# Attention feeding two gated layers: VectorE's copies, lower halves and a weight conversion moved between steps

## The chip, the core and the metric

The kernel runs on one core of a Trainium2 chip. The core has TensorE (matmuls, written to PSUM banks of 128 x 512 fp32), VectorE, ScalarE and GpSimd (elementwise work; GpSimd does not read PSUM here) and SyncE, which issues nearly all DMAs. Each engine works through its own list of instructions in order and waits on semaphores for the others. The metric is the device time of one execution in microseconds (us).

## What is computed

The reference is causal attention over 2 batches of 12 heads, 448 positions of 64, and two layers behind it, all in fp32:

```python
scores = scale * np.matmul(q, k.transpose(0, 1, 3, 2))
scores = np.where(mask, -1000000000.0, scores)
scores = scores - np.max(scores, axis=-1, keepdims=True)
attn = np.exp(scores)
attn = attn / (np.sum(attn, axis=-1, keepdims=True) + 1e-09)
x = np.matmul(attn, v)                      # heads joined: 896 x 768
x = (x @ w_a) * (x @ w_b) @ w_out           # d_ff 1536
h = x @ w_in                                # d_ff 2048
out = (h * (1.0 / (1.0 + np.exp(-h)))) @ w_out2
```

## The kernel before, in words

**Attention** is a hand-written pipeline of 30 steps (the loop at L705). Two heads make one unit `u`, 12 units in all, the first six of batch 0 (b = 0). A unit takes two steps, d = 2u (even, i = 0) and d = 2u + 1 (odd, i = 1). The queries of a unit are cut into seven chunks `j`; the even step handles chunks 6, 5, 0 (448, 384 and 64 keys), the odd one 4, 1, 3, 2. In a step TensorE does, in this order: the scores of unit u into banks `sc` (L568 and L572), a part of the product with v of an earlier unit (`xo`, L654, five steps later than its scores), and the transposes of normalized rows into two banks `pt` (L642, two steps later than their scores). Scores use a split of q and k in two parts: GpSimd makes the upper halves `qh`, `kh` (L538), VectorE the lower ones `ql`, `kl` (L543), in the odd step for the next unit.

For each chunk VectorE takes scores to `sm` with scale, mask and row minimum `nmax` (L591, one pool of three buffers, one for a group of chunks), ScalarE makes `p` = exp and its row sums (L595). A step later VectorE adds epsilon and inverts (`sums`, `rcp`, L604 and L605), and GpSimd multiplies `p` with it (L608). The step after that, TensorE transposes `p`; a step later still the banks `pt` are copied to `ptr` (L737 in the trace, where deferred work is called) by the table `COPIES`: those of an even step by one ScalarE and three VectorE copies, those of an odd one by three ScalarE copies. Transposes take their two banks from three, from unit 8 on from two (L621). Finished `xo` of a unit is cut in an upper part `xh` and a copy `xf` on ScalarE and a lower part `xl` on VectorE (L383 to L389).

**What sets the order.** `defer(k, prio, fn)` puts work k steps ahead; at the end of a step its list is sorted by `prio` and issued (L736). Before, ScalarE's copies have priority 0, `finish` of x 1, score work 2, VectorE's copies and `normalize` 3, and lower parts `xl` follow from `tasks`. Behind all that, a timeline issues steps of **weight conversion** by due time (L743). A granule of weights comes as 8-byte words; ScalarE makes `wr` from them (L213, L219), VectorE joins them to fp32 `wq` (L225, L230), then both make halves `wgah`/`wgal`, `wgbh`/`wgbl` (L252, L256). `CONV0`, `CONV1`, `CONV2` say in half steps over which stretch granules 0 and 1 are converted: 8 to 34 and 35 to 52. Sums of blocks of x (`S`, with halves `p3` to `p7`; L391) also run there, from step 22 on.

**After attention** come the layers, all matmuls `acc` of 448 columns (L295). Steps 24 to 27 already hold 36 matmuls of granule 0 on batch 0, the early products. Granule 0's other 36 follow attention, then 72 of granule 1, then granule 2 with halves `wah`, `wal`. The end of the kernel copies the last bank in two halves, on ScalarE and VectorE, and stores each (L933 to L938).

Of the kernel before, what the change touches and what calls it, by code (L numbers as in the profile page):

```python
# [24 lines left out]
    ((0, "scalar", 0, 2, 5, 2), (1, "vector", 2, 1, 5, 2), (1, "vector", 3, 1, 6, 1), (1, "vector", 0, 1, 0, 1)),  # L25
    ((0, "scalar", 0, 1, 1, 4), (1, "scalar", 1, 1, 2, 3), (1, "scalar", 2, 1, 4, 1)),
)
LAG_T = 2
# [3 lines left out]
CONV1 = 34  # L32
CONV2 = 52
# [6 lines left out]
A1 = 38  # L40
A2 = 11
# [21 lines left out]
def fused_kernel(ctx: ExitStack, tc: tile.TileContext, qk, v, w_ab, w_mid, w_in, w_out, out):  # L63
# [315 lines left out]
    def arrive(b, chunk, src):  # L379

        hi, lo = A.new(F32R, "xh"), A.new(F32R, "xl")
        XS[chunk, b] = hi, lo
        nc.scalar.copy(out=hi, in_=src)  # L383
        XF[chunk, b] = t = A.new(F32, "xf")
        nc.scalar.copy(out=t, in_=src)
        c, i = divmod(chunk, 2)
        if (b, i) != (1, 0):
            ACTS[{(0, 0): 1, (0, 1): 2, (1, 1): 4}[b, i]][c] = hi, lo
        return lambda: nc.vector.tensor_tensor(out=lo, in0=src, in1=hi[:].bitcast(F32), op=ALU.subtract)  # L389

    def sums_of(c):  # L391


        a11, a12, a21, a22 = (XF.pop((2 * c + i, b)) for b in range(B) for i in range(2))
# [11 lines left out]
        s3 = add("S", a11, a21, ALU.subtract)  # L406
        yield 2
# [69 lines left out]
    with tc.manual_schedule():  # L477

        with ExitStack() as actx:
# [6 lines left out]
            sm_p = sctx.enter_context(right(name="sm_p", bufs=3))  # L486
# [126 lines left out]
            def transposes(u, i):  # L613
# [11 lines left out]
                for n, copy, kb, nkb, j, nj in COPIES[i]:  # L625
                    size = nkb * nj * 2 * D
                    src = bank[n][:, o[n]:o[n] + size].rearrange("p (k h q) -> p k h q", k=nkb, h=2)
                    o[n] += size
                    dst = t["pt"][:, kb:kb + nkb, :, j * D:(j + nj) * D]
                    for a in range(nkb):  # L630
                        for c in range(nj):
                            place[j + c, kb + a] = src[:, a, :, c * D:(c + 1) * D]
                    if nkb == 1:
                        src, dst = src[:, 0], dst[:, 0]
                    if copy == "vector":
                        defer(1, 3, partial(nc.vector.tensor_copy, out=dst, in_=src))
                    else:
                        defer(1, 0, partial(nc.scalar.copy, out=dst, in_=src))
# [22 lines left out]
            tasks = []  # L661

            def finish(b, chunk, src):
                tasks.append(arrive(b, chunk, src))
                if b == 1 and chunk % 2:
                    sums_x.gens.append(sums_of(chunk // 2))
# [38 lines left out]
            for d in range(n_steps):  # L705
# [32 lines left out]
                while tasks:  # L738
                    tasks.pop(0)()
# [5 lines left out]
            for fn in sorted(late):  # L745
                for _, f in late[fn]:
                    f()
            while tasks:
                tasks.pop(0)()
# [126 lines left out]
        for at, g in enumerate(granules):  # L876
# [36 lines left out]
            def ending(b, i, acc, m=m, last=last):  # L913
# [19 lines left out]
                if last and b == 1 and i == 1:  # L933
                    o2, half = A.new(F32, "o2"), S // 2
                    nc.scalar.copy(out=o[:, 0:half], in_=src[:, 0:half])
                    nc.vector.tensor_copy(out=o2[:, 0:half], in_=src[:, half:S])
                    nc.scalar.dma_start(out=out[m + i, :, b * S:b * S + half], in_=o[:, 0:half])
                    nc.sync.dma_start(out=out[m + i, :, b * S + half:(b + 1) * S], in_=o2[:, 0:half])  # L938
                    A.free(o2)
                else:  # L940
                    nc.scalar.copy(out=o, in_=src)
                    nc.sync.dma_start(out=out[m + i, :, toks[b]], in_=o)
# [54 lines left out]
```

## Time and profile before

| | |
|---|---|
| time, median of 3 runs | 566.44 us (566.26 to 568.65) |
| the profiled execution: its time, its span | 566.35 us, 564.5 us |
| busy: TensorE, VectorE, ScalarE, GpSimd | 553.8, 426.6, 376.7, 72.8 us |
| granted TensorE clock | full speed in all slices |
| chain that ended last | TensorE 89%, of it 82% matmuls `acc`; VectorE 5% |

Busy time is a mean over very different stages: attention ends near 104 us, and GpSimd works only there. Matmuls overlap and their ends are modelled, so a busy TensorE need not be at its peak; how long the same instructions take in one place and in another says more. In brackets behind a timeline row stands how long the engine was idle before it, and who ended that.

### The profile page before, as it was taken

Reading aid. Unit: us, or ns where it says so; the run is one execution under the profiler, and the core shown is the slowest. Engines: PE = TensorE matmul, PEld = TensorE weight load, DVE = VectorE, ACT = ScalarE, POOL = GpSimd, SP = SyncE. Lnnn points to the kernel's source line nnn. Section 1 sums busy time; section 2 is a strip of 40 time slices with the busy share of each in tenths; the row PEclk is TensorE's granted clock in tenths of the full one; section 3 lists DMA queues with packets and bytes.
Section 4 is the critical chain, followed back from the end, with each engine's and each line's share of the span. In section 5 each row is a group of like instructions: output and inputs, shape, how many; then the busy total and the mean of one; then the engine's idle time right before and its main releaser. Section 6 shows DMA issues by size and latency. Waiting matters only on the chain.

```text
span 564.5 us, 8382 instructions
## 1 busy us (share of the span) xinstructions
PE 553.8 (98%) x2978; PEld 493.7 (87%) x2978; DVE 426.6 (76%) x818; ACT 376.7 (67%) x730; POOL 72.8 (13%) x127
## 2 busy tenths in 40 slices
PE   8999989999999999999999999999999999999997
PEld 6667757899999999999999999999999999999996
DVE  5899898688989898879683788888886797442500
ACT  4989988756666666678563675877776995632601
POOL 5888865000000000000000000000000000000000
PEclk9999999999999999999999999999999999999999
DMA  7346423033343433333333333333333242631501
GB/s 248 118 128 191 123 60 147 1 113 111 113 145 137 156 120 113 113 113 111 113 112 113 111 113 111 113 111 113 118 120 118 74 138 87 212 106 49 174 1 65
DMA packets 18234, 65.42 MB, mean 116 GB/s; under 512 B 2192, under 2 KB 6928, under 8 KB 18192
## 3 DMA queue, kind: packets, MB, share of 16 engines
q1 hardware_dynamic: 18048, 64.77, 34.1%
q8 instruction: 23, 0.38, 0.3%
q14 instruction: 19, 0.16, 0.1%
q10 hardware_dynamic: 144, 0.11, 0.1%
HBM read 62.13 MB, written 2.75 MB: 115 GB/s over the span
## 4 chain that ended last, share of the span: by engine, by line
PE 89%; DVE 5%; issue 2%; POOL 2%; ACT 1%; DMA 1%; SPq 0%; DVEq 0%; ACTq 0%; POOLq 0%
PE acc L295 82%; PE pt L642 2%; DVE sm L591 2%; PE sc L568 2%; POOL p L608 2%; PE xo L654 1%; PE sc L572 1%; DVE ptr L737 1%; DVE kl L543 1%; DMA k<-qk 1%; ACT p L595 0%; DVE sums L604 0%; ACT ptr L737 0%; SPq L526 0%; DVE wgal L256 0%
## 5 line engine op out<-in xcount | busy, mean ns | idle before, releaser
L225 DVE SCALAR_TENSOR_TENSOR wq<-wr 128x768 uint32<-128x768 uint32 (+1 forms) x76 | 66.3, 875 | 25.5 <-ACT wr L219 24.8
L318 ACT COPY s<-acc 128x448 f32<-128x448 f32 x72 | 38.5, 534 | 61.0 <-PE acc L295 60.6
L219 ACT ACTIVATE wr<-wr,wbias 128x768 uint32<-128x768 uint32 (+1 forms) x76 | 69.8, 918 | 0.0
L213 ACT ACTIVATE wr<-wr 128x768 f32<-128x768 f32 (+1 forms) x76 | 63.8, 839 | 2.5 <-DMA wr<-w_out 1.3
L230 DVE SCALAR_TENSOR_TENSOR wq<-wr,wq 128x768 uint32<-128x768 uint32 (+1 forms) x76 | 64.2, 877 | 0.1
L608 POOL TENSOR_SCALAR p<-p,rcp 128x448 f32<-128x448 f32 (+6 forms) x84 | 56.9, 693 | 19.5 <-DVE rcp L605 13.7
L595 ACT ACTIVATE p<-sm,nmax 128x448 f32<-128x448 f32 (+6 forms) x84 | 42.1, 514 | 13.0 <-DVE nmax L591 13.0
L295 PE MATMUL acc<-th,wgbl 128*128 128x448 f32 x168 | 49.5, 366 | 0.0
L295 PE MATMUL acc<-th,wgbh 128*128 128x448 f32 x168 | 49.4, 366 | 0.0
L295 PE MATMUL acc<-tl,wgah 128*128 128x448 f32 x168 | 49.4, 366 | 0.0
L295 PE MATMUL acc<-th,wgal 128*128 128x448 f32 x168 | 49.4, 365 | 0.0
L295 PE MATMUL acc<-tl,wgbh 128*128 128x448 f32 x168 | 49.4, 365 | 0.0
L295 PE MATMUL acc<-th,wgah 128*128 128x448 f32 x168 | 49.3, 365 | 0.0
L591 DVE CUSTOM_DVE_ANT_0 sm<-sc,mask 128x448 f32<-128x448 f32 (+6 forms) x84 | 31.2, 416 | 9.9 <-PE sc L572 7.5
L642 PE MATMUL pt<-ident,p 128*128 128x128 f32 x192 | 29.2, 284 | 6.0 <-DVE sums L604 2.4
L642 PEld LDWEIGHTS pt<-ident,p 128*128 128x128 f32 x192 | 20.6, 141 | 15.8 <-POOL p L608 7.5
L295 PEld LDWEIGHTS acc<-th,wgbh 128*128 128x128 f32 x168 | 31.5, 188 | 2.9 <-DVE s L788 0.2
L295 PEld LDWEIGHTS acc<-th,wgah 128*128 128x128 f32 x168 | 31.5, 188 | 2.8
L256 DVE TENSOR_TENSOR wgal<-wq,wgah 128x512 fp32r<-128x512 f32 (+1 forms) x20 | 16.4, 820 | 23.2 <-ACT wgah L252 14.3
L295 PEld LDWEIGHTS acc<-th,wgal 128*128 128x128 f32 x168 | 31.5, 188 | 2.5
L295 PEld LDWEIGHTS acc<-th,wgbl 128*128 128x128 f32 x168 | 31.5, 188 | 2.5
L295 PEld LDWEIGHTS acc<-tl,wgah 128*128 128x128 f32 x168 | 31.5, 188 | 2.5
(167 smaller groups left out, 1392.2 us busy)
## 6 DMA issues: line engine op xcount, KB each, us to landing
wr<-w_ab SPq DMA_DIRECT2D x24, 768.0 KB, 5.0
wr<-w_in SPq DMA_DIRECT2D x16, 768.0 KB, 5.2
wr<-w_out SPq DMA_DIRECT2D x24, 512.0 KB, 4.3
wr<-w_mid SPq DMA_DIRECT2D x12, 768.0 KB, 4.4
v<-v SPq DMA_DIRECT2D x12, 256.0 KB, 4.2
q<-qk SPq DMA_DIRECT2D x24, 112.0 KB, 3.1
k<-qk SPq DMA_DIRECT2D x12, 224.0 KB, 3.5
out<-o SPq DMA_DIRECT2D x11, 224.0 KB, 5.3
```

Of the source, the lines that this page charges most:

```text
L213: nc.scalar.activation(out=word(i, 1).bitcast(F32), in_=word(i, 1).bitcast(F32), func=AF.Copy, scale=2.0 ** -112)
L219: nc.scalar.activation(out=word(i, 0), in_=word(i, 0), func=AF.Relu, bias=wbias, scale=2.0 ** -29)
L225: nc.vector.scalar_tensor_tensor(out=xi(i), in0=word(i, 1), scalar=3, in1=word(i, 0), op0=ALU.logical_shift_left, op1=ALU.bitwise_or)
L230: nc.vector.scalar_tensor_tensor(out=xi(i), in0=word(i, 1), scalar=0x80000000, in1=xi(i), op0=ALU.bitwise_and, op1=ALU.bitwise_or)
L256: nc.vector.tensor_tensor(out=view[1], in0=src(), in1=view[0].bitcast(F32), op=ALU.subtract)
L295: nc.tensor.matmul(out=acc[:, 0:S], lhsT=w, rhs=a, start=first, stop=last, skip_group_check=True)
L318: nc.scalar.copy(out=t, in_=acc[:, 0:S])
L568: nc.tensor.matmul(out=sc, lhsT=t[a][:, j - BIG].rearrange("p h q -> p (h q)"), rhs=t[k][:, 0:K], start=(i == 0), stop=(i == 2))
L591: nc.vector.tensor_tensor_reduce(out=sm, in0=sc, in1=mask[:, S - K:S], op0=ALU.add, op1=ALU.min, scale=-(D ** -0.5), scalar=3.0e38, accum_ ...
L595: nc.scalar.activation(out=p_sb[u % 2][j][:, 0:K], in_=sm, func=AF.Exp, bias=t["nmax"][:, c:c + 1], scale=-1.0, accum_out=t["sums"][:, c:c ...
L608: nc.gpsimd.tensor_scalar(out=pj, in0=pj, scalar1=t["rcp"][:, COL[j]:COL[j] + 1], scalar2=1.0, op0=ALU.mult, op1=ALU.mult,)
L642: nc.tensor.transpose(out=place[j, kb], in_=p_sb[u % 2][j][:, kb * P:(kb + 1) * P], identity=ident)
```

## The change

- `COPIES`: the three copies of an even step's transposes that VectorE made go to ScalarE, and two of ScalarE's of an odd step go to VectorE (128 x 2 x 192 and 128 x 2 x 64). All have priority 0, so they are issued first in the step after their transposes.
- `xl` is no longer issued at the end of the step in which x is finished but one step later (`XL_STEPS`), behind `normalize`; so are the sums of x.
- For b = 0 ScalarE makes no `xf`; where the sums need it, VectorE adds `xh` and `xl` (`whole`).
- Granule 0 is converted over half steps 8 to 42, granule 1 over 43 to 62 (there are 60).
- Four buffers `sm` instead of three; the slot comes from another pool (`A1`, `A2`).
- The last bank is copied by one ScalarE copy and stored by one DMA.

```diff
 COPIES = (
-    ((0, "scalar", 0, 2, 5, 2), (1, "vector", 2, 1, 5, 2), (1, "vector", 3, 1, 6, 1), (1, "vector", 0, 1, 0, 1)),
-    ((0, "scalar", 0, 1, 1, 4), (1, "scalar", 1, 1, 2, 3), (1, "scalar", 2, 1, 4, 1)),
+    ((0, "scalar", 0, 2, 5, 2), (1, "scalar", 2, 1, 5, 2), (1, "scalar", 3, 1, 6, 1), (1, "scalar", 0, 1, 0, 1)),
+    ((0, "scalar", 0, 1, 1, 4), (1, "vector", 1, 1, 2, 3), (1, "vector", 2, 1, 4, 1)),
 )
+XL_STEPS = 1
...
-CONV1 = 34
-CONV2 = 52
+CONV1 = 42
+CONV2 = 62
...
-A1 = 38
-A2 = 11
+A1 = 37
+A2 = 12
...
-        XF[chunk, b] = t = A.new(F32, "xf")
-        nc.scalar.copy(out=t, in_=src)
+        if b:
+            XF[chunk, b] = t = A.new(F32, "xf")
+            nc.scalar.copy(out=t, in_=src)
...
+    def whole(chunk):
+
+        hi, lo = XS[chunk, 0]
+        t = A.new(F32, "xf")
+        nc.vector.tensor_tensor(out=t, in0=hi[:].bitcast(F32), in1=lo[:].bitcast(F32), op=ALU.add)
+        return t
+
     def sums_of(c):
-        a11, a12, a21, a22 = (XF.pop((2 * c + i, b)) for b in range(B) for i in range(2))
+        a21, a22 = (XF.pop((2 * c + i, 1)) for i in range(2))
+        a11, a12 = whole(2 * c), None
+        yield 1
...
         s3 = add("S", a11, a21, ALU.subtract)
+        yield 1
+        a12 = whole(2 * c + 1)
         yield 2
...
-            sm_p = sctx.enter_context(right(name="sm_p", bufs=3))
+            sm_p = sctx.enter_context(right(name="sm_p", bufs=4))
...
-                    if copy == "vector":
-                        defer(1, 3, partial(nc.vector.tensor_copy, out=dst, in_=src))
-                    else:
-                        defer(1, 0, partial(nc.scalar.copy, out=dst, in_=src))
+                    copy = nc.vector.tensor_copy if copy == "vector" else nc.scalar.copy
+                    defer(1, 0, partial(copy, out=dst, in_=src))
...
             def finish(b, chunk, src):
-                tasks.append(arrive(b, chunk, src))
+                defer(XL_STEPS, 4, arrive(b, chunk, src))
                 if b == 1 and chunk % 2:
-                    sums_x.gens.append(sums_of(chunk // 2))
+                    defer(XL_STEPS, 5, lambda: sums_x.gens.append(sums_of(chunk // 2)))
...
-                if last and b == 1 and i == 1:
-                    o2, half = A.new(F32, "o2"), S // 2
-                    nc.scalar.copy(out=o[:, 0:half], in_=src[:, 0:half])
-                    nc.vector.tensor_copy(out=o2[:, 0:half], in_=src[:, half:S])
-                    nc.scalar.dma_start(out=out[m + i, :, b * S:b * S + half], in_=o[:, 0:half])
-                    nc.sync.dma_start(out=out[m + i, :, b * S + half:(b + 1) * S], in_=o2[:, 0:half])
-                    A.free(o2)
-                else:
-                    nc.scalar.copy(out=o, in_=src)
-                    nc.sync.dma_start(out=out[m + i, :, toks[b]], in_=o)
+                nc.scalar.copy(out=o, in_=src)
+                nc.sync.dma_start(out=out[m + i, :, toks[b]], in_=o)
```

TensorE's and GpSimd's lists of instructions are the same in both kernels. On VectorE, this is the stretch before, from the second half of step 20 into step 21 (unit 10); `ISA` is the score operation, line 1 of the fence ends the joining of one half of granule 1's weights:

```order
L230 SCALAR_TENSOR_TENSOR wq<-wr,wq 128x768
L543 TENSOR_TENSOR ql<-q_120,qh 128x512
L543 TENSOR_TENSOR kl<-k,kh 128x448
L591 ISA sm,nmax<-sc,mask 128x320
L591 ISA nmax 128x1
L591 ISA sm,nmax<-sc,mask 128x128
L591 ISA nmax 128x1
L591 ISA sm,nmax<-sc,mask 128x256
L591 ISA nmax 128x1
L591 ISA sm,nmax<-sc,mask 128x192
L591 ISA nmax 128x1
L737 COPY ptr<-pt 128x2x128
```

The same stretch of VectorE in the changed kernel:

```order
L618 RECIPROCAL rcp<-sums 128x4
L391 TENSOR_TENSOR xl<-xo,xh 128x448
L556 TENSOR_TENSOR ql<-q_120,qh 128x512
L556 TENSOR_TENSOR kl<-k,kh 128x448
L604 ISA sm,nmax<-sc,mask 128x320
L604 ISA nmax 128x1
L604 ISA sm,nmax<-sc,mask 128x128
L604 ISA nmax 128x1
L604 ISA sm,nmax<-sc,mask 128x256
L604 ISA nmax 128x1
L604 ISA sm,nmax<-sc,mask 128x192
L604 ISA nmax 128x1
```

The conversions are gone from here, `xl` has come between `rcp` and `ql`, and no copies follow in that step.

On ScalarE, before, from the head of step 20 (copies of the odd step 19) into step 21:

```order
L737 COPY ptr<-pt 128x2x256
L737 COPY ptr<-pt 128x2x192
L737 COPY ptr<-pt 128x2x64
L595 ACTIVATE p_6_127,sums<-sm,nmax 128x448
L595 ACTIVATE p_5_126,sums<-sm,nmax 128x384
L595 ACTIVATE p_0_121,sums<-sm,nmax 128x64
L737 COPY ptr<-pt 128x4x128
L383 CAST xh<-xo 128x448
L385 COPY xf<-xo 128x448
```

The same stretch of ScalarE in the changed kernel:

```order
L746 COPY ptr<-pt 128x2x256
L608 ACTIVATE p_6_127,sums<-sm,nmax 128x448
L608 ACTIVATE p_5_126,sums<-sm,nmax 128x384
L608 ACTIVATE p_0_121,sums<-sm,nmax 128x64
L214 ACTIVATE wr<-wr 128x768
L746 COPY ptr<-pt 128x4x128
L746 COPY ptr<-pt 128x2x128
L746 COPY ptr<-pt 128x2x64 x2
L384 CAST xh<-xo 128x448
L387 COPY xf<-xo 128x448
```

Two copies have left the even step, three have joined the odd one, and a conversion step of granule 1 stands between them.

On VectorE behind the last copies of attention, in the changed kernel, while steps 28 and 29 and the first matmuls of the layers run:

```order
L391 TENSOR_TENSOR xl<-xo,xh 128x448
L397 TENSOR_TENSOR xf<-xh,xl 128x448
L257 TENSOR_TENSOR wgal<-wq,wgah 128x768
L409 TENSOR_TENSOR S<-xf 128x448
L415 TENSOR_TENSOR p7l<-S,p7h 128x448
L257 TENSOR_TENSOR wgbl<-wq,wgbh 128x768
L391 TENSOR_TENSOR xl<-xo,xh 128x448
```

Before, `wgal` and `wgbl` stood ahead of the last two `xl`, and there was no `xf` on this engine.

## Rows read from the trace of the kernel before

**Rows 1.** Chain that ended last, its end: start us, us, what.
```profile
103.97 457.16 PE acc L295 x2250
...
561.53 0.39 DVE o L936
```

**Rows 2.** Busy time by unit: stretch, length, then PE, PEld, DVE, ACT, POOL, ...
```profile
30.17:37.61 7.44, 7.31 (x60) 5.13 (x58) 7.37 (x25) 5.72 (x19) 6.62 (x9) 1.00 0.47 157
37.61:44.85 7.24, 6.88 (x58) 5.09 (x58) 7.17 (x28) 6.22 (x23) 5.92 (x9) 1.00 0.57 190
44.85:51.53 6.68, 6.68 (x59) 5.15 (x58) 6.28 (x28) 6.68 (x21) 5.23 (x9) 1.00 0.67 183
51.53:58.20 6.67, 6.67 (x60) 5.14 (x58) 6.60 (x26) 6.67 (x26) 5.93 (x9) 1.00 0.36 110
58.20:64.86 6.66, 6.66 (x59) 5.13 (x58) 6.63 (x25) 5.79 (x18) 5.92 (x9) 1.00 0.36 110
64.86:73.28 8.42, 7.16 (x59) 5.14 (x58) 6.42 (x28) 8.42 (x26) 5.62 (x10) 1.00 0.36 104
73.28:82.42 9.14, 7.10 (x59) 5.16 (x58) 8.88 (x29) 7.36 (x28) 7.32 (x10) 1.00 0.28 86
82.42:89.68 7.26, 6.88 (x59) 5.18 (x58) 5.95 (x25) 6.30 (x18) 4.10 (x8) 1.00 0.71 248
```

**Rows 3.** Timeline of TensorE: start us, us, instruction, [idle before it <- releaser].
```profile
22.50 0.98 PE L642 MATMUL pt<-ident,p 128*128 128x128 f32 x7 [0.39 <-ACT ptr L737]
...
40.64 0.66 PE L642 MATMUL pt<-ident,p 128*128 128x128 f32 x4 [0.36 <-POOL p L608]
...
67.84 1.32 PE L642 MATMUL pt<-ident,p 128*128 128x128 f32 x8 [0.89 <-ACT ptr L737]
...
81.71 0.95 PE L642 MATMUL pt<-ident,p 128*128 128x128 f32 x7 [2.01 <-DVE sums L604]
```

**Rows 4.** Timeline of VectorE in steps 20 and 21.
```profile
77.25 0.95 DVE L230 SCALAR_TENSOR_TENSOR wq<-wr,wq 128x768 uint32<-128x768 uint32 x1
...
80.76 0.81 DVE L737 COPY ptr<-pt 128x256 f32<-128x256 f32 x3
```

**Rows 5.** ScalarE to 104 us, grouped by form: count | busy us, mean ns | idle.
```profile
L385 ACT COPY xf<-xo 128x448 f32<-128x448 f32 x11 | 6.1, 552 | 0.0
L737 ACT COPY ptr<-pt 128x384 f32<-128x384 f32 x12 | 5.9, 492 | 0.0
...
L219 ACT ACTIVATE wr<-wr,wbias 128x768 uint32<-128x768 uint32 x4 | 4.1, 1023 | 0.0
L213 ACT ACTIVATE wr<-wr 128x768 f32<-128x768 f32 x4 | 3.7, 924 | 0.0
L737 ACT COPY ptr<-pt 128x128 f32<-128x128 f32 x12 | 3.4, 284 | 0.0
```

**Rows 6.** Timeline of VectorE and GpSimd in units 8 and 9.
```profile
61.47 0.91 DVE L543 TENSOR_TENSOR ql<-q,qh 128x512 fp32r<-128x512 f32 x1
...
61.82 2.62 POOL L608 TENSOR_SCALAR p<-p,rcp 128x320 f32<-128x320 f32 x4
...
65.09 0.59 DVE L389 TENSOR_TENSOR xl<-xo,xh 128x448 fp32r<-128x448 f32 x1
...
65.34 1.50 POOL L608 TENSOR_SCALAR p<-p,rcp 128x448 f32<-128x448 f32 x3 [0.90 <-DVE rcp L605]
```

**Rows 7.** Timeline behind attention: one instruction each of VectorE and TensorE for granule 2.
```profile
119.38 0.95 DVE L256 TENSOR_TENSOR wal<-wq,wah 128x768 fp32r<-128x768 f32 x1
...
126.01 0.36 PE L295 MATMUL acc<-xh,wah 128*128 128x448 f32 x1
```

**Rows 8.** DMA issues at the end: count, KB each, us from issue to landing.
```profile
out<-o SPq DMA_DIRECT2D x1, 224.0 KB, 1.9
...
out<-o SPq DMA_DIRECT2D x1, 112.0 KB, 1.7
```

**Rows 9.** Waits to 104 us: who for whom, us in total, times, longest.
```profile
ACT p L595 <- DVE nmax L591: 13.0, 10, 5.2
```

More of the change, by code (lines that the diff above doesn't have):

```diff
@@ L659, in pv @@
                     defer(1, 1, partial(finish, b, chunk, t["x"][:, 0:S]))
-            tasks = []
             def finish(b, chunk, src):
-                tasks.append(arrive(b, chunk, src))
+                defer(XL_STEPS, 4, arrive(b, chunk, src))
                 if b == 1 and chunk % 2:
-                    sums_x.gens.append(sums_of(chunk // 2))
+                    defer(XL_STEPS, 5, lambda: sums_x.gens.append(sums_of(chunk // 2)))
             wz = const.tile([P, P], F32, name="wz")
@@ L737, in fused_kernel @@
                     fn()
-                while tasks:
-                    tasks.pop(0)()
                 for n in range(2):
@@ L744, in fused_kernel @@
             run(fill)
[L745 to L749, printed above, removed]
+            while late:
+                now[0] = min(late)
+                for _, fn in sorted(late.pop(now[0]), key=lambda e: e[0]):
+                    fn()
         A.add(ctx.enter_context(tc.tile_pool(name="slots2", bufs=A3, reuse_waits="tile")), A3)
```

## The prediction

> **What bounds the kernel now.** I read the chain of waits first. From 103.97 us on it is one piece, 2250 matmuls of `acc` on TensorE without a gap, and behind it only two copies of the output [rows 1]. That tail runs in the same order in both kernels, so whatever this change is worth must appear ahead of 103.97, in attention. Next I read attention by units, a unit being one pair of heads, two steps, cut where TensorE starts the scores of 448 columns [rows 2]. TensorE runs the same instructions in each unit, yet its length differs: 6.68, 6.67 and 6.66 us in the three units from 44.85 to 64.86, where TensorE is busy throughout, and 7.44, 7.24, 8.42, 9.14 and 7.26 in others. I take 6.67 as what a unit costs TensorE, and the rest as waiting: 0.77 (30.17), 0.57 (37.61), 1.75 (64.86), 2.47 (73.28), 0.59 (82.42), together 6.15 us. The two units not shown, ahead of 30.17, are no longer than 7.0 each.
>
> Then I read who ends each wait, in TensorE's timeline [rows 3]. It is always the transposes, `pt`: at 22.50 and 67.84 they wait for a ScalarE copy that empties their bank (0.39 and 0.89), at 40.64 for GpSimd's `p` (0.36), at 81.71 for VectorE (2.01). That last one is named `sums`, but the instruction ahead of it on VectorE is the copy of `pt` that frees the bank: three copies from 80.76 on [rows 4]. From step 18 on transposes have two banks instead of three, so those of one step need both banks of the step before, and the copies stood behind two `wq`, `ql`, `kl` and four score chunks.
>
> **The change part by part.**
>
> Copies. VectorE's three copies in an odd step took 0.81 [rows 4]; they go to ScalarE, and stand ahead of that step's exponentials. ScalarE hands over its copies of 384 and 128 columns, which now stand at the head of VectorE's even step. ScalarE gives 0.49 + 0.28 and takes 0.28 twice and one of 256 columns, whose time lies between those of 128 and 384, 0.28 to 0.49, say 0.39 [rows 5]: +0.18 a unit by durations, between +0.07 and +0.28. TensorE's wait for VectorE goes, 2.01 at 81.71 and most of the shorter one of the next unit. Of 2.47 + 0.59 I count 3.0 as gone. What is late next in that place is ScalarE's copy; it is charged below.
>
> [...]
>
> `xf`. For the first batch the second copy of x goes: 0.55 less on ScalarE in six of twelve units [rows 5]. Six additions on VectorE replace it, late, from step 22 on, where `ql` and `kl` have ended. I cost those at nothing: TensorE has the early products there. If that cover were gone, two of them lie ahead of the last transposes, at about 0.6 each by `xl` [rows 6], which handles 448 columns too.
>
> Conversion. Granule 0 is stretched to step 21, granule 1 begins after that, so its four `wq` no longer share steps 19 to 21 with scores: part of the 2.47 above. On ScalarE, the wait of 1.75 in the unit from 64.86 belongs to four `wr` in steps 17 to 19, behind which the copies stood; they are gone from there. That unit has in ScalarE busy 8.42 of 8.42 [rows 2]. I take all 1.75 as recovered there.
>
> They come back in steps 20 to 22, though, with copies and `xf` beside them. In the three units from 44.85 to 64.86 ScalarE is busy 19.14 [rows 2] with three conversions at about 0.9, so 16.4 or 5.5 a unit without them; with the dearer copies 5.7. Three last units are 17.1, plus four `wr`, two at 0.92 and two at 1.02 [rows 5], 3.9: 21.0 against TensorE's 20.0. **I charge 1.0 us**; bounds are 0 (the lag fits the slack of one step) and 2.5 (it starts late by a conversion and meets the first copy every time).
>
> GpSimd. Waits of 0.77 and 0.57 come from `p` being late. Here a row shows why: the four `p` from 61.82 took 2.62 while `ql` ran from 61.47 and `kl` behind it; the three from 65.34 took 1.50 although `xl` ran from 65.09 to 65.68 [rows 6]. So `ql`, `kl` and `wq` hold GpSimd up, `xl` does not. `xl` now stands right behind `rcp`, ahead of `ql`, and gives the first `p` a stretch to run in; `rcp` itself comes earlier, since VectorE's odd step has lost 0.81 of copies and 0.59 of `xl` ahead of it. I count 1.34 as recovered. Against this, four even steps (8, 10, 16, 18) still hold a conversion between `xl` and `ql`: each can delay `p` by its own 0.95 [rows 4], with about as much gained from the earlier `rcp`. I charge 0.3 for the four, bounds 0 and 1.3.
>
> [...] If `xl` did block, its 0.59 would lengthen four even steps by as much again, and the sum would be 2.4 us less at most.
>
> Early part. The 0.39 at 22.50 goes, since the `wr` that kept ScalarE busy moved a step ahead. The first three steps are waits on the load and on GpSimd; nothing there moves.
>
> Score buffer. VectorE may run a whole step further ahead of ScalarE. I give it nothing of its own; it is what allows evened steps.
>
> Boundary. Granule 1 is now ready about when the tail starts; it is first read 36 matmuls later. `wal` of granule 2 starts at 119.38, and its first product at 126.01 [rows 7]: over 5 us of slack, of which some 1 to 3 are used (three additions and `wq` work now lie ahead). Cost nothing; if this cover is gone, TensorE stops by what is over.
>
> End. One copy of 448 columns replaces two halves. Before, the second half (0.39) began at 561.53 after the first [rows 1], so it ended at 561.92; a whole copy would end some 0.25 sooner, and its store takes 1.9 instead of 1.7 [rows 8]. Zero, within 0.1.
>
> **The sum.** 3.0 + 1.75 + 1.34 + 0.39 = 6.5 less 1.0 and 0.3 gives 5.2 us. The profiled execution took 566.35, span 564.5; the median of three is 566.44, so the profile stands for it. 566.35 - 5.2 = **561.1 us**, 0.9% faster. A measurement of this kernel tells about 0.5% (2.8 us) from no change.
>
> **Rivals.**
>
> *All of it comes back.* ScalarE's lag in steps 20 to 23 fits into TensorE's slack and conversions stay hidden: 566.35 - 6.5 = 559.8. For: in the early-product steps TensorE does not need the copies so soon. Against: 21.0 on 20.0.
>
> *ScalarE takes over.* Only VectorE's own wait goes, 2.0 and 0.4, and the ScalarE and GpSimd ones come back elsewhere: 564.0. For: ScalarE is busy 6.67 of 6.67 and 8.42 of 8.42 in two units [rows 2]. Against: it loses 0.55 in half of the units.
>
> *Slower: ScalarE's idle time stays and no longer fits.* It waited 13.0 us for `nmax` in ten waits, 5.2 of that once at the start [rows 9], so 7.8 over nine units, about 0.87 each. VectorE's scores now stand behind copies that wait for the last transposes, so this may grow. Nine units of ScalarE, six at 5.2 (no `xf`), three at 5.7 and ten conversions at 0.9, are 57.3; with 0.87 idle in each that is 65.1, a little under the 66.2 that the nine units from 16.24 to 82.42 take at present. It decides from 1.0 on; at 1.35 a unit it is 69.5, 3.3 more than now, so 569.6. Against: where ScalarE is behind, it is not idle (6.67 of 6.67), so the two do not add.
>
> *It does nothing.* Waits move to other steps in full, 566. For: units at 6.67 have VectorE at 6.6 already. Against: excess is in few units, each with its own cause.
>
> **How the numbers follow.** Forecast 0.54; all back 0.17; ScalarE takes over 0.18; slower 0.06; nothing 0.05. The two charges alone make 559.8 (both zero) to 563.7 (2.5 and 1.3); the takeover extends this to 564.0. The range 559.3 to 564.4 leaves out slower, nothing and the edges. Faster by over 0.5%, under 563.5: forecast, all back and a small part of the takeover, 0.73; within 0.5%: 0.20; slower 0.07.
>
> **What would show it.** Right: TensorE's 2.01 for VectorE is gone; units from 64.86 and 73.28 drop to 6.7 to 7.1; the tail starts near 98.7; `acc` remains about 457.2. GpSimd's `p` still shows waits at most of some tenths. What remains should be waits of `pt` for ScalarE's `ptr` near the last two score units. Wrong: units of 7.0 or more throughout (ScalarE takes over, or slower), or a gap of TensorE behind the start of the tail (boundary), or the same 2 us wait under another name.

## The result and the profile after

The changed kernel took **561.45 us** (median; 561.41 to 561.49), the kernel before 566.35 beside it: a ratio of 0.9905 (95%: 0.9879 to 0.9931), 4.9 us or 0.9% faster. The forecast was 561.1, within 559.3 to 564.4. The profiled execution took 561.41, its span 559.6. Busy now: TensorE 552.7, VectorE 427.8, ScalarE 375.3, GpSimd 72.2 us.

The end of the chain that ended last, against [rows 1] (start us, us, what; the second piece is from the same view of the last 20 us):

```profile
98.67 457.62 PE acc L296 x2250
...
556.31 0.53 ACT o L939
```

The tail is still one piece and begins 5.30 sooner (98.67 for 103.97). It is 0.46 longer, which I don't put down to the change: in the eleven experiments below where it is one piece too, it took 457.15 to 457.98. So 5.30 gained in attention are 4.9 in the time. The end is as good as unchanged: one copy of 0.53, where two halves stood.

Busy time by unit after, cut as in [rows 2] (stretch, length, TensorE, its weight loads, VectorE, ScalarE, GpSimd, ...):

```profile
29.17:35.84 6.67, 6.67 (x60) 5.14 (x58) 6.33 (x22) 5.67 (x23) 5.93 (x9) 1.00 0.37 111
35.84:42.63 6.79, 6.79 (x60) 5.12 (x58) 6.64 (x25) 5.45 (x21) 5.92 (x9) 1.00 0.45 139
42.63:49.35 6.72, 6.72 (x58) 5.11 (x58) 6.65 (x27) 5.91 (x23) 5.77 (x9) 1.00 0.79 260
49.35:56.24 6.89, 6.89 (x59) 5.12 (x58) 5.90 (x25) 6.89 (x26) 5.78 (x10) 1.00 0.54 157
56.24:62.91 6.67, 6.67 (x59) 5.14 (x58) 6.21 (x23) 5.63 (x19) 5.38 (x9) 1.00 0.34 108
62.91:69.58 6.67, 6.67 (x59) 5.12 (x58) 6.46 (x25) 5.86 (x21) 5.93 (x9) 1.00 0.46 133
69.58:76.26 6.68, 6.68 (x59) 5.15 (x58) 6.33 (x27) 6.68 (x24) 5.29 (x10) 1.00 0.15 39
76.26:84.26 8.00, 7.15 (x59) 5.16 (x58) 7.11 (x25) 8.00 (x25) 5.11 (x8) 1.00 0.37 129
```

These eight answer one to one to those of [rows 2]: 7.44, 7.24, 6.68, 6.67, 6.66, 8.42, 9.14, 7.26 have become 6.67, 6.79, 6.72, 6.89, 6.67, 6.67, 6.68, 8.00. Most of the waiting has left the middle (0.12, 0.05 and 0.22 over 6.67 remain in three units) and gathers in one unit, the last with scores, where ScalarE is busy 8.00 of 8.00. TensorE's timeline from 16 to 90 us shows three waits, where [rows 3] had six (four shown):

```profile
79.14 0.87 PE L653 MATMUL pt<-ident,p 128*128 128x128 f32 x6 [0.42 <-ACT ptr L746]
...
83.03 0.30 PE L653 MATMUL pt<-ident,p 128*128 128x128 f32 x1 [0.23 <-ACT ptr L746]
...
83.53 0.98 PE L653 MATMUL pt<-ident,p 128*128 128x128 f32 x7 [0.20 <-ACT ptr L746]
```

VectorE's 2.01 and GpSimd's 0.36 are gone; what is left in rows of this kind is for ScalarE's copies. Its timeline there says why:

```profile
77.60 1.03 ACT L220 ACTIVATE wr<-wr,wbias 128x768 uint32<-128x768 uint32 x1
78.50 0.59 ACT L746 COPY ptr<-pt 128x512 f32<-128x512 f32 x1
...
80.56 0.95 ACT L214 ACTIVATE wr<-wr 128x768 f32<-128x768 f32 x1
...
81.37 1.05 ACT L220 ACTIVATE wr<-wr,wbias 128x768 uint32<-128x768 uint32 x1
82.27 1.20 ACT L746 COPY ptr<-pt 128x512 f32<-128x512 f32 x4
```

The copies that free the banks stand behind `wr` of granule 1, one in the first case, two in the second. GpSimd waits less for `rcp`; the wait lists to 104 us, before and after, have (us in total, times, longest):

```profile
POOL p L608 <- DVE rcp L605: 13.7, 10, 3.3
```

```profile
POOL p L621 <- DVE rcp L618: 7.3, 8, 3.2
```

It waits more for ScalarE instead (in the same lists 2.8 us before and 5.3 after for `p`, 0.6 and 2.9 for `ptr`). What its earlier start was worth is taken up behind the experiments.

### The profile page after: what moved, and what is told of

Its sections match the earlier page's. It is cut to its first block, busy times and chain, and to the rows that moved or that the text cites. A ratio compares the mean times of both kernels' runs of the same rounds, so it can differ in the third digit from the quotient of the medians.

```text
span 559.6 us, 8368 instructions
## 1 busy us (share of the span) xinstructions
PE 552.7 (99%) x2978; PEld 493.6 (88%) x2978; DVE 427.8 (76%) x811; ACT 375.3 (67%) x736; POOL 72.2 (13%) x127
## 4 chain that ended last, share of the span: by engine, by line
PE 94%; DVE 3%; issue 1%; POOL 1%; ACT 1%; DMA 1%; SPq 0%; DVEq 0%; ACTq 0%; POOLq 0%
PE acc L296 83%; PE pt L653 4%; PE xo L665 3%; PE sc L581 3%; PE sc L585 2%; DVE sm L604 1%; POOL p L621 1%; DMA k<-qk 1%; DVE ql L556 0%; DVE kl L556 0%; ACT p L608 0%; ACT ptr L746 0%; DVE wgbl L257 0%; SPq L539 0%; DVE sums L617 0%
## 5 line engine op out<-in xcount | busy, mean ns | idle before, releaser
L296 PEld LDWEIGHTS acc<-tl,wgbh 128*128 128x128 f32 x168 | 31.5, 188 | 2.5
L653 PE MATMUL pt<-ident,p 128*128 128x128 f32 x192 | 27.8, 282 | 2.2 <-POOL p L621 1.3
```

The lines of the kernel that those rows point to most:

```text
L296: nc.tensor.matmul(out=acc[:, 0:S], lhsT=w, rhs=a, start=first, stop=last, skip_group_check=True)
L653: nc.tensor.transpose(out=place[j, kb], in_=p_sb[u % 2][j][:, kb * P:(kb + 1) * P], identity=ident)
```

## The experiments

Three theories. **A**, the prediction's: each part of the change cures waits of its own, at the price in the sum. **B**: the shifted conversion does nearly all, the copies nothing. **C**: the fourth buffer `sm` lets VectorE run ahead, and that is the gain. Since the start and the tail vary between executions (last section), I give beside each time the **attention length**, from the first transposes `pt` to the first `acc` of the tail in the profiled execution: 92.43 before (11.46 to 103.90), 87.08 after (11.51 to 98.60); these are differences of unrounded times, so a hundredth can be missing in the ones printed. Units are counted from 0: units 9, 10 and 11, the last three with scores, begin at 64.86, 73.28 and 82.42 in [rows 2], and the length of a unit is taken from one start of 448-column scores to the next.

### One part undone in the changed kernel

**The old conversion.**

```diff
-CONV1 = 42
-CONV2 = 62
+CONV1 = 34
+CONV2 = 52
```

> The changed kernel with both conversions back at their old half steps (8 to 34 and 35 to 52). Theory A, each wait has its own cause: ScalarE's four conversion instructions of granule 1 fall in steps 17 to 19 again and bring back the 1.75 us wait there, the joining on VectorE in steps 19 to 21 brings back some 0.8 of GpSimd's and VectorE's lateness, and the 1.45 us that TensorE now loses to ScalarE near steps 22 to 24 goes away: 562.5 us, between 561.8 and 563.5. Rival B, the later conversion alone made the gain: the 4.8 us of waits of steps 18 to 23 come back less 1.45, so 564.8 or more.

561.70 us (561.68 to 561.82), ratio 0.9914 [0.9900, 0.9927]; attention 87.61. Undoing it costs 0.25 by the medians, 0.5 by the profile. B falls. A had put more on it (its range began at 561.8), since the prediction counted the whole 1.75 as the conversion's: units 9 and 10 do lengthen, to 7.62 and 7.25, but most of that comes back where the changed kernel loses its 1.33.

**The old copies.** The old table `COPIES`, VectorE's copies at priority 3 again.

```diff
-                    copy = nc.vector.tensor_copy if copy == "vector" else nc.scalar.copy
-                    defer(1, 0, partial(copy, out=dst, in_=src))
+                    if copy == "vector":
+                        defer(1, 3, partial(nc.vector.tensor_copy, out=dst, in_=src))
+                    else:
+                        defer(1, 0, partial(nc.scalar.copy, out=dst, in_=src))
```

> The changed kernel with the table of copies and their priorities as before (three VectorE copies at the end of an odd step). Theory A: from step 18 on, with two banks, the transposes of each odd step wait for those copies again; without conversions ahead of them the wait is 0.3 to 0.6 in three steps instead of 2.0, and ScalarE's odd step is lighter: 562.5 us, between 561.9 and 563.5, with TensorE idle for VectorE's copies in odd steps from 19 on. Rival B, the later conversion alone made the gain: 561.4 us or a few tenths less.

564.05 us (563.85 to 564.41), 0.9956 [0.9943, 0.9968]; attention 89.85: 2.6 us, more than A expected (its range ended at 563.5). VectorE's timeline in step 19, then TensorE's, where the releaser is named `sums`, the instruction behind the copies, as in [rows 3]:

```profile
66.79 0.59 DVE L391 TENSOR_TENSOR xl<-xo,xh 128x448 fp32r<-128x448 f32 x1
...
67.30 1.02 DVE L257 TENSOR_TENSOR wgbl<-wq,wgbh 128x768 fp32r<-128x768 f32 x1
68.24 1.04 DVE L556 TENSOR_TENSOR ql<-q,qh 128x512 fp32r<-128x512 f32 x1
69.20 0.61 DVE L556 TENSOR_TENSOR kl<-k,kh 128x448 fp32r<-128x448 f32 x1
...
70.98 0.81 DVE L748 COPY ptr<-pt 128x256 f32<-128x256 f32 x3
```

```profile
71.93 0.96 PE L655 MATMUL pt<-ident,p 128*128 128x128 f32 x7 [1.42 <-DVE sums L617]
```

That is [rows 4] with other work ahead of the copies: `wgbl` of granule 0, which the new stretch has put there, instead of two `wq`. With the old copies, then, the shifted conversion moves VectorE's wait from unit 10 to unit 9 (8.64 long here), because `wgbl`, `ql` and `kl` stand ahead of the copies at the end of that odd step.

**`xl` at the end of its own step.** `arrive(...)` and the sums go back to a list that is called behind the deferred work of the same step.

```diff
-                defer(XL_STEPS, 4, arrive(b, chunk, src))
+                tasks.append(arrive(b, chunk, src))
...
```

> The changed kernel with the lower halves of x back in the step in which x is finished. Theory A: GpSimd's first product no longer runs under xl between rcp and ql, so it comes 0.5 later in even steps, which costs where a conversion stands there too (steps 8, 10, 16, 18): 562.0 us, between 561.5 and 562.8. Rival: the place of xl costs nothing, 561.4 within 0.2.

562.42 us (562.26 to 563.15), 0.9928 [0.9916, 0.9941]; attention 87.94. About 0.9, where A expected 0.6 with a range up to 1.4. More than half of it is in unit 4 (steps 8 and 9), which takes 7.14 instead of 6.67; there the weight loads of the transposes (PEld in the profile) wait for GpSimd's `p` three times, 1.0 us in all.

**Three buffers `sm`.**

```diff
-            sm_p = sctx.enter_context(right(name="sm_p", bufs=4))
+            sm_p = sctx.enter_context(right(name="sm_p", bufs=3))
...
```

> The changed kernel with three score buffers as before. Theory A: the buffer has no gain of its own, 561.4 us to 561.8. Rival C, the fourth buffer is what lets VectorE run ahead: 563 us or more, with VectorE waiting for ScalarE's exponentials.

561.29 us (560.85 to 561.66), 0.9908 [0.9892, 0.9923]; attention 87.16. The fourth buffer is worth nothing here; C falls.

**`xf` on ScalarE for both batches**, and no additions in `whole`.

```diff
-        if b:
-            XF[chunk, b] = t = A.new(F32, "xf")
-            nc.scalar.copy(out=t, in_=src)
+        XF[chunk, b] = t = A.new(F32, "xf")
+        nc.scalar.copy(out=t, in_=src)
```

> The changed kernel with the second copy of x on ScalarE for both batches, as before, and no additions for it on VectorE. ScalarE has 0.43 to 0.55 more in six of the odd steps, 7 to 17, in which it is not behind in the changed kernel except at step 14: 561.4 to 562.0 us. If ScalarE were the bound throughout, 6 x 0.5 = 3 us more, 564.4.

561.40 us (561.30 to 562.04), 0.9906 [0.9884, 0.9929]; attention 87.30. Worth 0.2 at most, undone alone.

**The same, with `xl` from the copy `xf`** instead of from `xo`: two inputs in SBUF instead of one in PSUM.

```diff
-        return lambda: nc.vector.tensor_tensor(out=lo, in0=src, in1=hi[:].bitcast(F32), op=ALU.subtract)
+        return lambda: nc.vector.tensor_tensor(out=lo, in0=t, in1=hi[:].bitcast(F32), op=ALU.subtract)
```

> As the kernel with the second copy of x on ScalarE for both batches, but the lower half of x is computed from that copy, so that xl has both inputs in SBUF instead of one in PSUM. If only VectorE instructions with two inputs in SBUF hold GpSimd up, the first p of even steps no longer runs under xl: 320-column p of 0.53 us become 0.9 to 1.4 or start later, and TensorE waits for GpSimd 0.1 to 0.5 in the even steps with a conversion: 0.5 to 2 us more than its twin. If the inputs' place does not matter, the two are equal within 0.2 us and the 320-column p stay at 0.53.

562.92 us (562.72 to 563.47), 0.9931 [0.9911, 0.9951]; attention 88.64, 1.34 more than in the run before. GpSimd and VectorE from 16 to 90 us, grouped by form (count, busy us, mean ns, idle), first with `xl` from PSUM, then from SBUF:

```profile
L617 POOL TENSOR_SCALAR p<-p,rcp 128x320 f32<-128x320 f32 x11 | 7.9, 721 | 5.3 <-ACT p7h L410 1.8 <-ACT ptr L742 1.5 <-ACT p L604 1.2
...
L390 DVE TENSOR_TENSOR xl<-xo,xh 128x448 fp32r<-128x448 f32 x9 | 5.3, 594 | 0.0
```

```profile
L617 POOL TENSOR_SCALAR p<-p,rcp 128x320 f32<-128x320 f32 x11 | 15.6, 1417 | 5.0 <-DVE rcp L614 2.3 <-ACT p7h L410 1.7 <-ACT p L604 1.0
...
L390 DVE TENSOR_TENSOR xl<-xf,xh 128x448 fp32r<-128x448 f32 x9 | 6.6, 729 | 0.0
```

The first `p` of an odd step's rows, which runs beside `xl`, takes 1.42 us instead of 0.72, and `xl` itself 0.73 instead of 0.59. The four `p` of such a group together lose less: in the same two views the 128-column ones fall from 1.11 to 0.89 and the 256-column ones from 0.71 to 0.48, by my reading because those behind the first meet less of `ql`, which these views do not show. TensorE feels it: from 16 to 104 us the weight loads of its transposes wait for GpSimd's `p` 6.2 us in 16 waits, where it was 3.6 in 8. The prediction read out of [rows 6] that `xl` does not hold GpSimd up. These two runs show it for `xl` from PSUM (0.72 for the `p` beside it), and not for `xl` with both inputs in SBUF (1.42). (Such an `xl` also has to wait for `xf`, 0.4 behind `xh`, but VectorE shows no idle time ahead of it.) The prediction had priced this case, `xl` blocking GpSimd, at 2.4 us at most; here it costs 1.3 to 1.5.

### One or two parts alone in the kernel before

**The conversion alone**, 8 to 42 and 43 to 62.

```diff
-CONV1 = 34
-CONV2 = 52
+CONV1 = 42
+CONV2 = 62
```

> The kernel before with the two conversions at the new half steps (8 to 42 and 43 to 62) and nothing else changed. Theory A, each wait has its own cause: ScalarE's wait of 1.75 us in unit 9 goes, and of the 2.5 in unit 10 the 1.9 that the two joining steps stood ahead of VectorE's copies; GpSimd's 1.34 stays, and 1.0 comes back as ScalarE's lateness in steps 20 to 23: 566.35 - 1.75 - 1.9 + 1.0 = 563.7 us, between 563.0 and 564.7. Rival B, the later conversion alone made the gain: 562 us or less.

563.88 us (563.52 to 565.11), 0.9950 [0.9932, 0.9968]; attention 89.95. Alone it is worth 2.5, undone alone 0.5: its gain and that of other parts overlap.

A's 563.7 is met here by luck. Of its terms, the 1.9 of unit 10 came true (9.14 became 7.24) and a part of the 1.0 for ScalarE, but unit 9, from which 1.75 should have gone, still takes 8.28 instead of 8.42. It now waits for VectorE's copies, with `wgbl` ahead of them as in the run with the old copies:

```profile
71.62 0.96 PE L642 MATMUL pt<-ident,p 128*128 128x128 f32 x7 [1.42 <-DVE sums L604]
```

What makes up for it was not in the expectation: units 2, 3 and 4 (from 16.24, 23.24 and 30.17 before) are shorter by 0.78, 0.26 and 0.44.

**The copies alone**, the new table at priority 0.

```diff
-    ((0, "scalar", 0, 2, 5, 2), (1, "vector", 2, 1, 5, 2), (1, "vector", 3, 1, 6, 1), (1, "vector", 0, 1, 0, 1)),
-    ((0, "scalar", 0, 1, 1, 4), (1, "scalar", 1, 1, 2, 3), (1, "scalar", 2, 1, 4, 1)),
+    ((0, "scalar", 0, 2, 5, 2), (1, "scalar", 2, 1, 5, 2), (1, "scalar", 3, 1, 6, 1), (1, "scalar", 0, 1, 0, 1)),
+    ((0, "scalar", 0, 1, 1, 4), (1, "vector", 1, 1, 2, 3), (1, "vector", 2, 1, 4, 1)),
```

> The kernel before with the new table of copies, all first in their step, and nothing else changed. Theory A: TensorE's 2.0 for VectorE at step 21 and most of the 0.6 of step 23 go, ScalarE's wait in unit 9 grows a little under its dearer odd step: 566.35 - 2.6 + 0.4 = 564.1 us, between 563.4 and 565.2. Rival B: 566 us, the copies do not matter while the conversion stays where it was.

566.19 us (565.93 to 566.80), 0.9993 [0.9982, 1.0004]; attention 92.27. Nothing: A is wrong on this part, which in the changed kernel is the dearest of all; the expectation's rival B had this time. TensorE's waits (us, times, longest), and its two worst units, 9 and 10:

```profile
PE pt L640 <- ACT ptr L735: 2.9, 6, 1.4
PE pt L640 <- DVE ptr L735: 0.6, 2, 0.3
PE pt L640 <- POOL p L608: 0.3, 1, 0.3
```

```profile
64.34:73.37 9.03, 7.18 (x59) 5.14 (x57) 5.46 (x23) 9.03 (x27) 6.37 (x12) 1.00 0.30 97
73.37:81.48 8.11, 7.34 (x59) 5.13 (x58) 7.98 (x25) 6.79 (x25) 5.99 (x7) 1.00 0.19 46
```

VectorE's wait of 2.01 is gone, and ScalarE has taken its place: 8.42 [rows 2] has become 9.03, with ScalarE busy in all of it. TensorE's worst wait and what ScalarE did ahead of it (first line: in the step before):

```profile
60.54 0.67 ACT L595 ACTIVATE p<-sm,nmax 128x448 f32<-128x448 f32 x1 [0.69 <-DVE nmax L591]
...
66.73 1.00 ACT L219 ACTIVATE wr<-wr,wbias 128x768 uint32<-128x768 uint32 x1
67.60 0.59 ACT L735 COPY ptr<-pt 128x512 f32<-128x512 f32 x1
```

```profile
68.25 0.87 PE L640 MATMUL pt<-ident,p 128*128 128x128 f32 x6 [1.38 <-ACT ptr L735]
```

ScalarE first waits for `nmax`, since on VectorE `xl`, `wgbl` and its new copies stand ahead of the scores, and a few us later it is late with a conversion ahead of the copy.

The question was then which other part makes the copies pay. Three runs, on one chip:

**The copies and `xl` a step later** (the two edits above, with the sums a step later too and the end copy of the change; conversion, `xf` and `sm` as before).

```diff
-                tasks.append(arrive(b, chunk, src))
+                defer(XL_STEPS, 4, arrive(b, chunk, src))
```

> The kernel before with the new copy table (both kinds at priority 0), `xl` and the sums one step later, and the whole copy at the end; the conversion, ScalarE's `xf` for both batches and three buffers `sm` stay as before. The new copies alone gave nothing (566.19, unit 9 of 9.03 us with ScalarE busy 9.03), and with everything but the conversion 561.7. Theory A: ScalarE is late in unit 9 and only less work on ScalarE (`xf` gone) makes the copies pay: here 565.5 to 566.5. Theory B: VectorE's odd step is what makes both late, since `xl` stands behind the conversions and ahead of nothing that needs it, while the score work behind it is what ScalarE's exponentials wait for: moving `xl` makes the copies pay, here 562.0 to 563.0. If neither, it is the fourth `sm`, and both this and the next stay above 565.

563.12 us (563.10 to 563.50), 0.9943 [0.9930, 0.9955]; attention 88.66: just above the second range.

**The copies, and no `xf` of the first batch on ScalarE**, again with the end copy of the change, and with the additions of `whole` on VectorE.

```diff
-        XF[chunk, b] = t = A.new(F32, "xf")
-        nc.scalar.copy(out=t, in_=src)
+        if b:
+            XF[chunk, b] = t = A.new(F32, "xf")
+            nc.scalar.copy(out=t, in_=src)
```

> The same, but `xl` stays at the end of its own step, and ScalarE's `xf` of the first batch is dropped instead (VectorE adds the halves later). Theory A: 562.0 to 563.0. Theory B: 565.5 to 566.5.

564.32 us (564.25 to 565.08), 0.9965 [0.9953, 0.9978]; attention 90.47: between the two ranges. Against the copies alone, `xl` is worth 3.1 by the medians and `xf` 1.9. So both theories of these two runs hold in part, the second (that moving `xl` is what makes the copies pay) in the larger one; neither excludes the other. The same wait of TensorE in the two runs, `xl` moved and `xf` dropped:

```profile
66.08 0.88 PE L649 MATMUL pt<-ident,p 128*128 128x128 f32 x6 [0.45 <-ACT ptr L742]
```

```profile
66.72 0.88 PE L653 MATMUL pt<-ident,p 128*128 128x128 f32 x6 [0.91 <-ACT ptr L748]
```

1.38 became 0.45 and 0.91. ScalarE's waits for `nmax` fell from 6.4 us to 3.4 with `xl` moved, and not without `xf` (6.9): the one takes idle time out of ScalarE's list, the other work. For the worst wait the rows show how. With `xl` moved, ScalarE's list ahead of it reads:

```profile
58.17 0.67 ACT L604 ACTIVATE p<-sm,nmax 128x448 f32<-128x448 f32 x1 [0.30 <-DVE nmax L600]
...
65.42 0.61 ACT L742 COPY ptr<-pt 128x512 f32<-128x512 f32 x1
```

From that exponential to the copy ScalarE has no wait of over 0.15 us in either run, and takes 7.25 us here and 7.06 (60.54 to 67.60) with the copies alone. What differs is the start: 1.67 us into its unit here (which begins at 56.50), 2.90 there (57.64).

**The copies and the conversion.**

```diff
-CONV1 = 34
-CONV2 = 52
+CONV1 = 42
+CONV2 = 62
```

> The kernel before with two parts of the change together: the new copies and the new stretches of conversion; `xl`, `xf`, `sm` as before. Alone the first gave 566.19 and the second 563.88. If the copies pay as soon as unit 9 has no conversions in it, they give here most of the 2.6 us that undoing them in the changed kernel costs: 562.0 to 562.7 (`xl` late is worth 0.85 in the changed kernel, and is missing). If they need `xl` or `xf` moved too: 563.5 to 564.2.

563.36 us (562.94 to 563.83), 0.9947 [0.9934, 0.9959]; attention 89.45. Just under the second expectation: on top of the conversion the copies are worth 0.5 by either measure. Units 9 and 10 are at 6.67 here, but units 4 and 7 take 7.43 and 7.42 (at 53.09 TensorE waits 0.54 for `ptr`), and unit 11 waits for `ptr` too. So a unit 9 free of conversions is not enough; with `xl` moved as well, in the changed kernel, units 4 and 7 take 6.67 and 6.89.

### A conversion later still

Granule 1 from half step 48 to 66, so that its four `wr` stand behind the last exponentials.

```diff
-            line.convert(granules[1], (CONV1 + 1 - 2 * n_steps) * SLOT_MM, (CONV2 - CONV1) * SLOT_MM)
+            line.convert(granules[1], (48 - 2 * n_steps) * SLOT_MM, 18 * SLOT_MM)
```

> The changed kernel with granule 1's conversion begun at half step 48 and ended at 66 (43 to 62 in the change), so that all four of its `wr` on ScalarE stand behind the last exponentials. In the changed kernel the last score unit is 1.33 us too long, and its transposes wait for ScalarE's `ptr`, behind such `wr`. If those are the cause: attention shorter by 0.9 to 1.3, 560.1 to 560.6. If it is the dearer copies and `xf` that make ScalarE late there, or if the joins and halves, now later on VectorE, stop TensorE at granule 1: 561.2 or more.

561.37 us (560.94 to 561.40), 0.9908 [0.9895, 0.9922]: no faster than the change. Yet attention took 85.58, 1.50 less. The last score unit:

```profile
76.21:82.88 6.67, 6.67 (x60) 5.14 (x58) 6.14 (x24) 6.15 (x24) 4.17 (x8) 1.00 0.40 107
```

No wait is left in it, so granule 1's conversion was its 1.33. The edit moves VectorE's share of it too, but what TensorE waited for there was ScalarE's `ptr`, behind the `wr`. TensorE stops behind attention instead:

```profile
127.17 0.47 PE L296 MATMUL acc<-p7h,wbh 128*128 128x448 f32 x1 [0.31 <-ACT s L319]
...
129.67 0.47 PE L296 MATMUL acc<-p3h,wdh 128*128 128x448 f32 x1 [0.41 <-ACT s L319]
```

and ScalarE's timeline shows the copy `s`, which empties a bank of `acc`, behind the conversion of granule 3:

```profile
125.30 0.84 ACT L253 CAST wah<-wq 128x768 fp32r<-128x768 f32 x1 [2.42 <-DVE wq L231]
126.17 0.51 ACT L253 CAST wdh<-wq 128x384 fp32r<-128x384 f32 x1
126.59 0.53 ACT L319 COPY s<-acc 128x448 f32<-128x448 f32 x1
```

ScalarE stood 2.42 us at a conversion that waits for VectorE, with `s` queued behind it. In the changed kernel `s` at 126.49 waits for TensorE. Counted from one matmul's start to the next, the two stops took 0.67 and 0.78 where 0.205 is usual, 1.04 in all. Of the 0.46 that remained, 0.25 is still there at the end of the last matmul in the profiled execution and 0.08 in the medians; no run shows what took the rest. So the time fell in the second range of the expectation, though attention did as the first said, and TensorE stops in granule 2's products, not in granule 1's.

## Why the prediction was right, and where not

The waits over 6.67 us a unit, before and after, with the two units ahead of [rows 2]. Those were, before:

```profile
16.24:23.24 7.00, 6.61 (x51) 4.75 (x50) 5.80 (x27) 7.00 (x21) 5.45 (x10) 1.00 0.46 129
23.24:30.17 6.93, 6.89 (x59) 5.12 (x57) 5.69 (x22) 6.93 (x24) 5.56 (x9) 1.00 0.27 88
```

and after, the first of them (the second is 6.67):

```profile
16.29:22.50 6.21, 6.21 (x50) 4.72 (x50) 5.45 (x22) 5.64 (x20) 5.25 (x10) 1.00 0.40 122
```

| step of the prediction | forecast | measured |
|---|---|---|
| early part, units from 16.24 and 23.24 | 0.39 | 7.00 + 6.93 to 6.21 + 6.67: 1.05 |
| GpSimd, next three units | 1.34, less 0.3 | 7.44 + 7.24 + 6.68 to 6.67 + 6.79 + 6.72: 1.18 |
| VectorE and ScalarE, last three score units | 3.0 + 1.75 | 8.42 + 9.14 + 7.26 less 3 x 6.67: 4.81 to be had, with what ScalarE takes of it in the next row |
| ScalarE late in steps 20 to 23 | 1.0 | 1.33 in the last unit, 0.12 behind it, and 0.22 in the unit from 49.35: 1.67 |
| sum | 5.2 | 5.37 by units; 5.30 by the start of the tail, with a start 0.05 later |

**The place of the bound, the unit cost and the order of the steps held.** 6.67 (once 6.68) is what a unit takes in four of the eight rows; the tail started at 98.67, where 98.7 was forecast; the remaining waits are ScalarE's `ptr` in the last score unit; the boundary showed no gap: `wal` of granule 2 now starts at 115.11 and its first product stands at 120.77, 5.7 us apart where [rows 7] have 6.6.

**Terms that were mis-sized.** *ScalarE's charge* was 1.67 for 1.0. For 1.45 of it the mechanism and the place were right, and the later conversion shows it, since without those four `wr` the unit is 6.67. The other 0.22 was charged nowhere: in the unit from 49.35, with ScalarE busy 6.89 of 6.89, the transposes' weight loads (L653, from 51 to 52.3 us) wait for the copy that stands behind `wgah` of granule 0:

```profile
  ACT ptr L746: 0.2, 1
```

The working of the charge compared mean work of three units with TensorE's; what counted was that single copies stand behind one or two `wr` of 0.95 to 1.05. *The early part* was 1.05 for 0.39: I took only the wait that stands in brackets in [rows 3], though ScalarE was busy 7.00 of 7.00 and 6.93 of 6.93 in those units. Short waits leave no row (the shortest shown is 0.15 us); the length of the unit shows them. With the conversion alone these two units took 6.22 and 6.67. *GpSimd* came to 0.16 of new waits for 0.3. That the sum is so near is luck: 0.66 and 0.14 more was gained than forecast in the first two rows and 0.06 in the third, and 0.67 less in the last.

**GpSimd's term came near its size, but one of its reasons did not hold.** The prediction gave the first `p` behind `xl` a stretch to run in, and an earlier `rcp`. In unit 4 the transposes waited for the four `p` of an odd step's rows, in unit 5 for the three of an even step's. These groups, before and after:

```profile
34.04 3.32 POOL L608 TENSOR_SCALAR p<-p,rcp 128x320 f32<-128x320 f32 x4
38.69 2.19 POOL L608 TENSOR_SCALAR p<-p,rcp 128x448 f32<-128x448 f32 x3 [1.33 <-DVE rcp L605]
```

```profile
32.19 3.32 POOL L621 TENSOR_SCALAR p<-p,rcp 128x320 f32<-128x320 f32 x4 [0.41 <-DVE rcp L618]
36.46 1.50 POOL L621 TENSOR_SCALAR p<-p,rcp 128x448 f32<-128x448 f32 x3 [0.95 <-ACT p L608]
```

The group of four, the one behind which `xl` now stands, is no shorter: its first `p` runs free, but the next ones meet more (from 16 to 90 us the 320-column `p` fell from a mean of 1.44 to 0.68, the 128-column one rose from 0.53 to 1.16). It begins earlier, 3.02 us into its unit instead of 3.87. The group of three begins earlier as well (0.62 instead of 1.08), and it is shorter: before, VectorE did a `wq` beside it (from 38.95), now copies and scores. So the earlier `rcp` held; the free stretch that shortened a group lies in the other one than the prediction had it.

**The step that failed is the assignment to parts.** The prediction gave each wait to one part: the 3.0 to the copies, the 1.75 to the conversion. Attention lengths say otherwise:

| parts of the change in it | attention, us | time, us |
|---|---|---|
| none | 92.43 | 566.35 |
| copies | 92.27 | 566.19 |
| copies, `xf` | 90.47 | 564.32 |
| conversion | 89.95 | 563.88 |
| all but copies | 89.85 | 564.05 |
| copies, conversion | 89.45 | 563.36 |
| copies, `xl` | 88.66 | 563.12 |
| all but `xl` | 87.94 | 562.42 |
| all but conversion | 87.61 | 561.70 |
| all but `xf` | 87.30 | 561.40 |
| all but the fourth `sm` | 87.16 | 561.29 |
| all | 87.08 | 561.45 |

The copies are worth 0.2 alone and 2.8 last; the conversion 2.5 alone and 0.5 last; `xl` 3.6 on top of the copies and 0.9 last. By removing VectorE's wait the copies make ScalarE the late engine, and what `xl`, `xf` or the conversion then take out of ScalarE's list pays. Nor is the 1.75 the conversion's alone: with it and the old copies unit 9 still takes 8.28, and VectorE is the late engine there. The whole came out right all the same, because with all parts in place no such second cause was left in units 9 and 10 (6.67 and 6.68). The takeover rival (the wait comes back on ScalarE) is thus true of the copies alone, with 566.2 rather than 564.0. In the full change it is only the charge of 1.67. The prediction named ScalarE's idle time for `nmax` under its slower rival and let it go; moving `xl` takes it from 6.4 to 3.4 us, and in unit 9, 1.02 us shorter by it, the rows above show this path. In the rest of the 3.6 GpSimd has a share: the transposes' weight loads waited for its `p` 6.8 us from 16 to 104 us with the copies alone and 4.6 with `xl` moved, for ScalarE's `ptr` 3.5 and 2.1. No run separates the two in TensorE's time.

## What to carry to other kernels

In a stage like this one, where several engines share a fixed order and are busy most of the time, a wait can belong to a place rather than to one instruction: here, with the conversion alone, ScalarE's wait of 0.89 us in unit 9 was gone, and VectorE's of 1.42 stood in the same unit. So cost the parts of such a change as a set, by each engine's list over the same steps, and judge a part by undoing it as well as by doing it alone. Read the length of a repeated unit, and the waits of the weight loads, before the waits in brackets, and, before moving work past the end of a stage, see what is queued behind it in the next one.

## What the runs showed of the hardware

The first 28 score matmuls took from 3.34 us to 4.15 in the executions profiled, in no relation to the edits: 3.65 before, 3.66 after, and here in the two runs on `xl`'s source, whose lists of matmuls are the same (TensorE's timeline):

```profile
5.20 3.34 PE L581 MATMUL sc<-k,q 128*64 128x448 f32 x28 [0.64 <-DMA k<-qk]
```

```profile
5.00 4.15 PE L581 MATMUL sc<-k,q 128*64 128x448 f32 x28 [0.17 <-DMA k<-qk]
```

The granted clock reads full speed in both, and six of the fourteen profiles show 3.34 here. The difference lies at the start: the first four of these matmuls, of 448 columns, took 0.54 to 0.56 us each in the first run and 0.95 to 0.98 in the second, while those of 256 columns took 0.38 in both. I have no cause that a run shows. It is why the experiments are compared by attention length, which begins behind it, and why differences of under half a microsecond between single profiles mean little.
